# Linear attention and a GELU layer on one core: a planner that models two GpSimd stops, and a last half block in other PSUM banks

## The chip, the cores and the metric

The kernel runs on one core of one Trainium2 chip. The metric is the device time of one execution in microseconds (us), as the median of several runs. All times in the profile count from the first instruction of one profiled execution; the span is the time from its first to its last instruction. PE is TensorE, DVE is VectorE, ACT is ScalarE, POOL is GpSimd and SP is SyncE, which here issues all transfers.

## The reference

Eight batches of eight heads of linear attention (576 positions, 64 wide, 128 features) give 4608 tokens of 512 values, and these go through two matrix products with an exact GELU between them (512 to 2048 to 512):

```python
def phi(x):
    proj = np.einsum('bhsd,df->bhsf', x, w_phi)
    proj = proj - np.max(np.abs(proj), axis=-1, keepdims=True)
    return np.concatenate([np.exp(proj), np.exp(-proj)], axis=-1)
q_p, k_p = (phi(q), phi(k))
kv = np.einsum('bhsf,bhsd->bhfd', k_p, v)
z = np.sum(k_p, axis=2)
num = np.einsum('bhsf,bhfd->bhsd', q_p, kv)
den = np.einsum('bhsf,bhf->bhs', q_p, z)[..., None] + 1e-06
x = (num / den).transpose(0, 2, 1, 3).reshape(4608, 512)
h = x @ w_in
g = 0.5 * h * (1.0 + erf(h / sqrt(2)))
out = g @ w_out
```

All data are float32. The matrix products are kept accurate by splitting each operand into a high and a low part and adding three of the four partial products.

## The kernel before

**Stages.** The first part of the program mixes two things. The *attention* goes batch by batch and pair of heads by pair: `pk` and `pq` are the projections of k and q, `mx` (DVE) and `mb` (POOL, an all-reduce over partitions, line L550) their absolute maxima, `ek` and `ef` the exponentials (ACT), `kv` the sums over positions, `kvn` a copy of them, `pn` the numerators and `xo` their copy, which is written to HBM as `x_d`. The denominators go by matmuls `pd` and a copy `do` for the first two batches, and later by `un` (DVE) and an all-reduce `db` on POOL (line L592). They go to HBM as `d_d`; DVE takes their quotients in `dc`, which are written to HBM as `r_d`. The *blocks* are the two matrix products. Eight plain blocks (j = 0 to 7, 256 tokens each) load `x_d` into `xl` and `r_d` into `rb`, multiply and split them into `xh` and `xl`, and then for each of eight units u do 24 matmuls into `ph_j_u`, two GELUs on ACT, one subtraction `gl_j_u` on DVE, and 12 matmuls into `po_j`. The weights `w_i` and `w_o` are loaded as float64 bit patterns and converted on DVE (`wt_i`, `wt_o`, lines L362 to L368) during the first 200 us.

Five wide blocks (j = 4 to 8 in units of 512 tokens) then do the same with seven products for each 2 x 2 block multiplication instead of eight. Their first product goes into `pa` and `pb` and reads operands from HBM, `s_d` (sums of weights) and `o_d` (plain weights), through a ring of eight slots, two in each of the tiles `w_o0`, `w_o4`, `w_o8` and `w_o12`, which the plain blocks no longer need then (loads at line L860). The inputs of a wide block are loaded into `xr` and `wbp` (lines L807 and L811). Its second product is done for two halves m = 0 and 1. For each half, eight units add 7 x 3 matmuls into seven sums, M1 to M7, from the operands `gs` and `sp`; then the seven sums are added up into four output quarters and written out (line L963).

**PSUM.** The banks are tags of one pool: `pp` (two banks), `kv`, `pn`, `ph` (two) and `po` (two banks in one tile). The seven sums of a half block stand in `po` (M1, M2, M4, M5) and the two `pp` (M6, M7 and M3). One half must therefore be added up before the next may start in the same banks.

**What sets the order.** The function `fused_kernel` does not issue instructions; it describes operations to a planner (`Plan`), each with an engine, a cost, a rank (a due time) and its buffers. `Plan.order` then plays the program once: of the operations that can start next on each engine it takes the one of lowest rank, and sets its start and end. Instructions are issued in the order of these starts. The planner thus fixes the row of instructions of every engine, among them SP, where a transfer that must wait for its buffer holds up all that stand behind it. Due times come from constants at the end of the file: `T15` sets the pace of the blocks, `CR` and `CSPAN` when the sums of weights are due, and so on.

The planner knows that GpSimd can stop VectorE. In the kernel before, when an all-reduce starts at t, any VectorE instruction without an operand in PSUM is taken not to start before t + `LOCK_MAX` (1.4 us, for a maximum) or t + `LOCK_SUM` (2.4 us, for a sum):

```python
if o.eng == "dve" and not o.psum and taken and taken[-1][0] <= t < taken[-1][1]:
    t = taken[-1][1]
...
taken.append((t, t + (LOCK_MAX if cost < 3.0 else LOCK_SUM)))
```

All matmuls stand at line L315 of the profile, all two-operand instructions of DVE at L345, all copies on ACT at L339, since helpers record them.

## Time and profile before

| | |
|---|---|
| median of 3 runs | 1074.14 us (1073.64 to 1078.09) |
| profiled execution | 1074.69 us, of which the span is 1072.8 us |
| PE busy | 1041.4 us, 97% of the span |
| DVE / ACT / POOL busy | 827.5 (77%) / 671.6 (63%) / 327.1 (30%) us |
| mean granted clock of PE | 0.994 of full speed |

A line of the profile's timeline reads: start in us, length in us, engine, line, operation, written tile <- read tiles, shapes, number of instructions drawn together; in brackets the idle time of the engine just before it, and what ended it. The table of stretches gives, for each stretch of the span, the busy time of each engine in it. The chain of waits follows the work that ended last back through what released it; its pieces have a start, a length and a name. Tile names are shortened there: `w_o` stands for all of `w_o0` to `w_o14`.

### The profile page before, as it was taken

How to read it: one execution, taken by the hardware profiler on the slowest of the kernel's cores; microseconds unless marked ns; L12 is line 12 of the kernel's file. 1: busy time of each engine (PE TensorE's matmuls, PEld its weight loads, DVE VectorE, ACT ScalarE, POOL GpSimd, SP SyncE). 2: the span in 40 equal slices, each digit the busy share in tenths (PEclk: the TensorE clock that was granted, in tenths of full speed). 3: DMA queues.
4: the chain of work that ended last, by engine and by line, in shares of the span. 5: the costliest groups of instructions: out<-in, count | busy, mean ns of one | idle time of the engine just before them, and what ended most of it. 6: DMA issues, size and time to landing. Idle time of an engine off the chain costs nothing.

```text
span 1072.8 us, 24540 instructions
## 1 busy us (share of the span) xinstructions
PE 1041.4 (97%) x9578; PEld 911.5 (85%) x9578; DVE 827.5 (77%) x1588; ACT 671.6 (63%) x1236; POOL 327.1 (30%) x116
## 2 busy tenths in 40 slices
PE   7898999999999999999999999999999999999997
PEld 4666777778787887888788898899999999999997
DVE  5999999557787467668769869768778788787784
ACT  5997878778777777878686434444354454354351
POOL 1452045565676566676573100000000000000000
PEclk9999999999999999999999999999999999999999
DMA  7888852324214223223114771998668768766621
GB/s 274 286 295 258 268 143 88 89 70 123 76 54 134 75 68 114 68 63 96 55 48 137 194 227 47 300 284 267 207 206 262 216 201 271 217 193 207 204 78 40
DMA packets 178643, 174.33 MB, mean 162 GB/s; under 512 B 29168, under 2 KB 164784, under 8 KB 176480
## 3 DMA queue, kind: packets, MB, share of 16 engines
q1 hardware_dynamic: 178528, 172.76, 52.5%
q8 instruction: 76, 1.25, 0.5%
q14 instruction: 39, 0.32, 0.1%
HBM read 138.83 MB, written 33.89 MB: 161 GB/s over the span
## 4 chain that ended last, share of the span: by engine, by line
PE 75%; DVE 14%; DMA 5%; issue 2%; ACT 2%; SPq 1%; POOL 1%; DVEq 0%; ACTq 0%; POOLq 0%
PE po L315 29%; PE ph L315 13%; PE pb L315 10%; PE pa L315 7%; PE kv L315 5%; PE pn L315 5%; PE pk L315 4%; PE pq L315 3%; DVE tt L345 2%; DVE mx L494 1%; DVE gl L345 1%; DVE ek L345 1%; DVE wt_o L366 1%; DVE pc L345 1%; POOL db L592 1%
## 5 line engine op out<-in xcount | busy, mean ns | idle before, releaser
L592 POOL PARTITION_ALL_REDUCE db<-un x48 | 178.1, 3710 | 137.2 <-DVE un L589 117.9
L315 PE MATMUL ph<-xh,w_i 128*128 128x256 f32 x1024 | 201.3, 285 | 2.6 <-DVE gl L345 2.6
L550 POOL PARTITION_ALL_REDUCE mb<-pc x64 | 151.5, 2375 | 134.6 <-ACT pc L339 128.4
L315 PEld LDWEIGHTS ph<-xh,w_i 128*128 128x128 f32 x1024 | 163.8, 188 | 12.4 <-issue 6.7
L315 PE MATMUL po<-w_o,gh 128*128 128x512 f32 x512 | 163.5, 400 | 0.2 <-ACT ob L339 0.2
L315 PE MATMUL ph<-xl,w_i 128*128 128x256 f32 x512 | 144.3, 282 | 0.0
L315 PE MATMUL pb<-b,w_o 128*128 128x256 f32 x936 | 132.8, 282 | 2.6 <-DMA w_o<-o_d 2.2
L315 PEld LDWEIGHTS pb<-b,w_o 128*128 128x128 f32 x936 | 120.4, 190 | 3.0 <-DMA w_o<-o_d 2.4
L315 PE MATMUL po<-t,sp 128*128 128x256 f32 x720 | 110.1, 280 | 2.5 <-DVE ob L345 2.1
L315 PEld LDWEIGHTS po<-w_o,gh 128*128 128x128 f32 x512 | 90.2, 188 | 25.3 <-issue 9.1
L315 PEld LDWEIGHTS kv<-vt,ek 128*64 128x64 f32 x2560 | 85.0, 140 | 26.1 <-issue 8.9
L315 PE MATMUL pa<-b,w_o 128*128 128x256 f32 x702 | 101.8, 282 | 0.5 <-DVE gl L345 0.5
L315 PE MATMUL po<-w_o,gl 128*128 128x512 f32 x256 | 101.1, 395 | 0.0
L315 PEld LDWEIGHTS ph<-xl,w_i 128*128 128x128 f32 x512 | 96.6, 189 | 1.8
L315 PEld LDWEIGHTS po<-t,sp 128*128 128x128 f32 x720 | 95.6, 188 | 2.9 <-issue 2.3
L315 PE MATMUL kv<-vt,ek 128*64 128x65 f32 x2560 | 91.8, 226 | 4.9 <-ACT kvn L339 3.0
L345 DVE TENSOR_TENSOR g<-g 128x128 f32<-128x128 f32 x320 | 91.3, 288 | 5.9
L494 DVE TENSOR_REDUCE mx<-pk 128x4 f32<-128x512 f32 (+2 forms) x90 | 51.6, 576 | 55.8 <-PE pk L315 53.0
L502 ACT ACTIVATE ek<-ek 128x512 f32<-128x512 f32 (+1 forms) x140 | 81.8, 589 | 18.1 <-DVE ek L345 16.2
L315 PEld LDWEIGHTS pa<-b,w_o 128*128 128x128 f32 x702 | 91.3, 190 | 0.8 <-DVE gl L345 0.7
L339 ACT CAST gs<-g 128x384 fp32r<-128x384 f32 x80 | 41.0, 513 | 75.7 <-PE po L315 75.4
L556 ACT ACTIVATE ef<-pc 128x576 f32<-128x576 f32 x128 | 81.4, 679 | 10.6 <-DVE pc L345 7.4
(102 smaller groups left out, 1973.7 us busy)
## 6 DMA issues: line engine op xcount, KB each, us to landing
w_o<-s_d SPq DMA_DIRECT2D x156, 256.0 KB
w_o<-o_d SPq DMA_DIRECT2D x117, 256.0 KB
vt<-in_va_dram SPq DMA_DIRECT2D x32, 325.0 KB
kt<-in_kT_dram SPq DMA_DIRECT2D x16, 576.0 KB
qt<-in_qT_dram SPq DMA_DIRECT2D x64, 144.0 KB
x_d<-xo SPq DMA_DIRECT2D x64, 144.0 KB
out_dram<-ob SPq DMA_DIRECT2D x36, 256.0 KB
raw_i<-in_w_in_dram SPq DMA_DIRECT2D x8, 1024.0 KB
```

What stands on the lines that cost most here:

```text
L315: return tc.keep_in_program_order(nc.tensor.matmul(*a, **kw))
L339: op(eng, cost, lambda: nc.scalar.copy(out=dst(), in_=src()), r=r, w=w, **kw)
L345: op(eng, cost, lambda: e.tensor_tensor(out=dst(), in0=a(), in1=b(), op=o), r=r, w=w, **kw)
L366: op("dve", dve(1024), lambda: v.scalar_tensor_tensor(out=t(), in0=low(), scalar=29, in1=t(), op0=ALU.logical_shift_right, op1=ALU.bitwise ...
L494: op("dve", dve(128 * n * nj, True), lambda view=view, mx=mx, js=js: nc.vector.tensor_reduce(out=mx()[:, 0].rearrange("p (j i) -> p j i", ...
L502: op("act", act(256 * n, inside), lambda at=at, es=es, s=s: nc.scalar.activation(es[s](), at(), AF.Exp, scale=1.0 - 2.0 * s), r=[parts[0][ ...
L550: op("pool", 2.35, lambda mb=mb, pc=pc: nc.gpsimd.partition_all_reduce(mb(), pc(), P, bass_isa.ReduceOp.absmax), r=[pc], w=[mb], **k(1))
L556: op("act", act(2 * HS), lambda ef=ef, pc=pc, s=s: nc.scalar.activation(ef()[:, s], pc(), AF.Exp, scale=1.0 - 2.0 * s), r=[pc], w=[ef], ta ...
L592: op("pool", 3.85, lambda db=db, un=un: nc.gpsimd.partition_all_reduce(db(), un(), P, bass_isa.ReduceOp.add), r=[un], w=[db], **k())
```

## The change

**The planner's model of VectorE and GpSimd.** Each operation gets a `port`: 0 where it is not on VectorE or has an operand in PSUM, 1 otherwise, 2 for a fast instruction with a single large input (marked by a class `Fast`). An all-reduce now starts at the later of t + 0.13 and the end of a running VectorE instruction, and records two spans: in the first, from its start to 1.1 us before its end, operations of port 1 and 2 wait; in the second, from 0.85 or 0.9 to 0.2 or 0.15 us before its end, those of port 2 wait. The costs of the two all-reduces are 2.28 and 3.6 us instead of 2.35 and 3.85.

```diff
-            if o.eng == "dve" and not o.psum and taken and taken[-1][0] <= t < taken[-1][1]:
-                t = taken[-1][1]
+            if o.port and taken:
+                held = taken[-1]
+                if held[0] <= t < held[1]:
+                    t = held[1]
+                if o.port == 2 and held[2] <= t < held[3]:
+                    t = held[3]
             return t
...
+            if o.eng == "dve":
+                port[0] = o.port
             if o.eng == "pool":
-                taken.append((t, t + (LOCK_MAX if cost < 3.0 else LOCK_SUM)))
+                at = max(t + 0.13, clock["dve"] - 0.02 if port[0] else 0.0)
+                cost += at - t - 0.13
+                end = t + cost
+                taken.append((at, end - (1.11 if o.cost < 3.0 else 1.13), end - (0.85 if o.cost < 3.0 else 0.9), end - (0.2 if o.cost < 3.0 else 0.15)))
```

**A dependence.** A buffer `said` without storage makes the planner place the first wide block's first casts `gs` behind the last plain block's two output copies on ACT.

**The last half block** (j = 8, m = 1). Its seven sums stand in four banks of the tags `ph`, `ph`, `kv` and `pn`: M1 and M2, M4 and M5, M6 and M7, M3. In its last unit the products come in the order 1, 2, 6, 7, 5, 4, 3, and the sums are added up one by one as they are finished, with three output transfers instead of two.

```diff
-            po0 = ps["po"]([P, 4, TB], F32, f"po_{j}_{m}")
-            po1 = [ps["pp"]([P, 2, TB], F32, f"po_{j}_{m}_{n}") for n in range(2)]
...
+            late = j == NBLK // 2 - 1 and m == 1
+            if late:
+                banks = [ps[tag]([P, 2, TB], F32, f"po_{j}_{m}_{n}") for n, tag in enumerate(("ph", "ph", "kv", "pn"))]
+                place = {n: (banks[i // 2], i % 2) for i, n in enumerate((1, 2, 4, 5, 6, 7, 3))}
...
-                for at, n in enumerate((1, 2, 4, 5, 6, 7, 3)):
+                for at, n in enumerate((1, 2, 6, 7, 5, 4, 3) if late and u == NU - 1 else (1, 2, 4, 5, 6, 7, 3)):
...
-                    op("pe", 3 * mm_cost(128, TB), go, r=[xt, wt], w=[bank], rank=lag(u + at / 7))
+                    op("pe", 3 * mm_cost(128, TB), go, r=[xt, wt], w=[part[n]], also=[bank], rank=lag(u + at / 7))
...
+            if late:
...
+                copy("act", act(TB, True), v1, M[1], [part[1]], [v], also=k["also"], rank=k["rank"])
+                add(c11, v1, M[2], [part[2], v], [left])
...
+                add(v1, v1, M[6], [part[6], v], [v])
+                add(u3, v1, M[7], [part[7], v], [right])
+                add(v1, v1, M[5], [part[5], v], [v])
+                for i, n in ((1, 5), (0, 4)):
+                    add(lambda i=i, ob=ob: ob[1]()[:, i], u3, M[n], [part[n], right], [low])
...
+                add(u3, v1, M[3], [part[3], v, low], [right])
```

**Constants.** Some twenty due times and thresholds get other values; two of them:

```diff
-CSPAN = 106.117
+CSPAN = 147.298
-T15 = 853.69
+T15 = 848.682
```

The matmuls and their number stay the same. The order of every engine changes, since the planner plays with other costs and due times. Three places are shown, always the instructions of the kernel before and then those of the changed kernel; the line numbers of the two files differ (L315 and L329 are the same matmul helper, L345 and L359 the same DVE helper, L860 and L875 the same load).

On PE, where the first half of the last block ends and the second begins (`po_8_0` are sums of the first half, `po_8_1` of the second; the last number of a name counts buffers). Before:

```order
L315 MATMUL po_8_0_0_12899<-t_3_1_8216,sp_8_0_7_13300 128x256 x3
L315 MATMUL po_8_0_0_12899<-t_3_0_8197,sp_8_0_7_13300 128x256 x3
L315 MATMUL po_8_0_1_12935<-w_o14_2208,sp_8_0_7_13300 128x256 x3
L315 MATMUL po_8_1_0_13343<-t_0_1_7801,sp_8_1_0_13318 128x256 x3
L315 MATMUL po_8_1_0_13343<-t_0_0_7790,sp_8_1_0_13318 128x256 x3
L315 MATMUL po_8_1_0_13343<-t_0_1_7801,sp_8_1_1_13186 128x256 x3
```

After:

```order
L329 MATMUL po_8_1_0_13313<-w_o2_838,gs_8_1_0_13280 128x256 x3
L329 MATMUL po_8_1_1_13324<-t_0_1_7807,gs_8_1_0_13280 128x256 x3
L329 MATMUL po_8_1_0_13313<-w_o0_666,gs_8_1_1_13131 128x256 x3
L329 MATMUL po_8_1_0_13313<-w_o2_838,gs_8_1_1_13131 128x256 x3
L329 MATMUL po_8_0_12908<-t_3_0_8190,sp_8_0_7_13300 128x256 x3
L329 MATMUL po_8_0_0_12899<-t_3_1_8211,sp_8_0_7_13300 128x256 x3
L329 MATMUL po_8_0_0_12899<-t_3_0_8190,sp_8_0_7_13300 128x256 x3
L329 MATMUL po_8_0_1_12935<-w_o14_2159,sp_8_0_7_13300 128x256 x3
L329 MATMUL po_8_1_1_13324<-t_0_1_7807,gs_8_1_1_13131 128x256 x3
```

Products of the second half, which have banks of their own now, stand ahead of the last four of the first half.

On SP, at the change-over from the plain to the wide blocks (`xr_5` and `wbp` are inputs of the second wide block, `w_o0` to `w_o12` the ring of operands of the first). Before:

```order
L860 DMA w_o8_1699<-o_d0_379 128x2x256
L860 DMA w_o8_1699<-s_d0_7120 128x2x256
L807 DMA xr_5_0_8153<-x_d4_0_3920 128x4x32
L811 DMA wbp_94<-r_d4_0_4693 64x2x32 x2
L807 DMA xr_5_0_8153<-x_d4_1_3960 128x4x224
L811 DMA wbp_94<-r_d4_1_4803 64x2x224 x2
L807 DMA xr_5_1_8167<-x_d4_1_3960 128x4x64
L807 DMA xr_5_1_8167<-x_d5_0_4780 128x4x192
L860 DMA w_o12_2122<-o_d0_379 128x2x256
L860 DMA w_o12_2122<-o_d1_1115 128x2x256
```

After:

```order
L875 DMA w_o8_1642<-o_d0_470 128x2x256
L875 DMA w_o8_1642<-s_d0_6952 128x2x256
L875 DMA w_o12_2014<-o_d0_470 128x2x256
L875 DMA w_o12_2014<-o_d1_1019 128x2x256
L875 DMA w_o0_666<-s_d1_7101 128x2x256 x2
L822 DMA xr_5_0_8179<-x_d4_0_3778 128x4x32
L826 DMA wbp_94<-r_d4_0_4519 64x2x32 x2
L822 DMA xr_5_0_8179<-x_d4_1_3908 128x4x224
L826 DMA wbp_94<-r_d4_1_4641 64x2x224
L875 DMA w_o4_1252<-s_d1_7101 128x2x256
```

Four loads of the ring moved ahead of the loads of `xr_5_0`; the load of `w_o4` stands behind the `wbp` loads now.

On DVE, ahead of the subtraction `gl` of unit 6 of the first plain block. Before:

```order
L345 TENSOR_TENSOR ek_2_1_3_0_2009<-pk_2_1_3_1930,mx_2_1_3_1939 128x512
L364 TENSOR_SCALAR wt_o12_1895<-wt_o12_1895 128x1024
L362 TENSOR_SCALAR wt_o14_1996<-wt_o14_1996 128x1024
L366 SCALAR_TENSOR_TENSOR wt_o12_1895<-raw_o12_1701,wt_o12_1895 128x1024
L494 TENSOR_REDUCE mx_2_1_4_2067<-pk_2_1_4_2048 128x4
L586 TENSOR_SCALAR un_2_0_1_2071<-ef_2_0_1_1970,kvn_2_0_0_1368 128x288
L368 SCALAR_TENSOR_TENSOR wt_o12_1895<-raw_o12_1701,wt_o12_1895 128x1024
L586 TENSOR_SCALAR un_2_0_1_2071<-ef_2_0_1_1970,kvn_2_0_0_1368 128x288
L345 TENSOR_TENSOR pc_2_1_0_2041<-pc_2_1_0_2041,mb_2_1_0_2051 128x576
L589 SCALAR_TENSOR_TENSOR un_2_0_1_2071<-ef_2_0_1_1970,kvn_2_0_0_1368,un_2_0_1_2071 128x288
L364 TENSOR_SCALAR wt_o14_1996<-wt_o14_1996 128x1024
L345 TENSOR_TENSOR gl_0_6_2124<-ph_0_6_2023,gh_0_6_2087 128x512
```

After:

```order
L359 TENSOR_TENSOR ek_2_1_1_0_1931<-pk_2_1_1_1860,mx_2_1_1_1921 128x512
L376 TENSOR_SCALAR wt_o12_1888<-wt_o12_1888 128x1024
L378 TENSOR_SCALAR wt_o12_1888<-wt_o12_1888 128x1024
L600 TENSOR_SCALAR un_2_0_1_1976<-ef_2_0_1_1926,kvn_2_0_0_1522 128x288
L380 SCALAR_TENSOR_TENSOR wt_o12_1888<-raw_o12_1676,wt_o12_1888 128x1024
L600 TENSOR_SCALAR un_2_0_1_1976<-ef_2_0_1_1926,kvn_2_0_0_1522 128x288
L382 SCALAR_TENSOR_TENSOR wt_o12_1888<-raw_o12_1676,wt_o12_1888 128x1024
L359 TENSOR_TENSOR gl_0_6_2012<-ph_0_6_1934,gh_0_6_1996 128x512
```

The first steps of `wt_o14`, the subtraction `pc_2_1_0` and part of `un_2_0_1` moved from before this `gl` to behind it.

## Rows read from the trace of the kernel before

**Rows 1.** Stretches: from:to, length, busy us (instructions) of each engine, clock, DMA

```profile
0.00:180.00 180.00, 159.71 (x1833) 117.27 (x1834) 161.63 (x229) 146.06 (x258) 65.49 (x28) 0.98 0.72 232
180.00:660.00 480.00, 479.73 (x4373) 394.53 (x4372) 350.53 (x576) 343.59 (x570) 261.61 (x88) 1.00 0.34 99
...
150.00:180.00 30.00, 27.03 (x217) 22.30 (x218) 29.97 (x33) 24.36 (x37) 19.26 (x6) 1.00 0.40 113
...
660.00:690.00 30.00, 27.33 (x195) 25.97 (x194) 24.22 (x56) 14.78 (x34) 0.00 (x0) 0.94 0.68 203
```

**Rows 2.** Waits of PE: for what, us in total, times, longest

```profile
PE ph L315 <- DVE gl L345: 2.6, 2, 1.4
PE pn L315 <- ACT do L339: 2.4, 1, 2.4
...
PE pb L315 <- DMA w_o<-o_d: 2.2, 1, 2.2
PE po L315 <- DVE ob L345: 2.1, 1, 2.1
...
PE pa L315 <- DVE gl L345: 0.5, 1, 0.5
...
PE po L315 <- DVE sp L345: 0.4, 1, 0.4
```

**Rows 3.** Timelines of POOL, DVE and PE between 150 and 171 us

```profile
150.53 4.19 POOL L592 PARTITION_ALL_REDUCE db<-un  x1 [5.53 <-DVE un L589]
...
151.57 2.41 DVE L364 TENSOR_SCALAR wt_o<-wt_o 128x1024 uint32<-128x1024 uint32 x1
153.90 1.37 DVE L362 TENSOR_SCALAR wt_o<-wt_o 128x1024 f32<-128x1024 f32 x1
...
160.82 0.67 DVE L364 TENSOR_SCALAR wt_o<-wt_o 128x1024 uint32<-128x1024 uint32 x1
...
162.15 0.39 PE L315 MATMUL ph<-xh,w_i 128*128 128x256 f32 x1 [1.42 <-DVE gl L345]
...
170.12 0.39 PE L315 MATMUL ph<-xh,w_i 128*128 128x256 f32 x1 [1.20 <-DVE gl L345]
```

**Rows 4.** Chain of waits, 60 to 100 us: start, length, what

```profile
73.33 6.12 DMA r_d<-dc
```

**Rows 5.** Timelines of SP and PE at the change-over

```profile
652.05 0.54 SPq L860 DMA_DIRECT2D w_o<-s_d  x1
666.47 0.38 SPq L807 DMA_DIRECT2D xr<-x_d  x1
...
671.38 1.21 SPq L860 DMA_DIRECT2D w_o<-o_d  x2
...
665.40 0.39 PE L315 MATMUL po<-w_o,gl 128*128 128x512 f32 x1
```

**Rows 6.** Chain of waits, 655 to 690 us

```profile
671.38 4.99 DMA w_o<-o_d
...
677.38 2.38 PE pa L315 x12
679.76 2.08 PE pb L315 x12
...
683.99 1.42 PE pb L315 x12
```

**Rows 7.** Timeline where the last half block begins

```profile
1047.60 1.66 PE L315 MATMUL po<-t,sp 128*128 128x256 f32 x12 [2.12 <-DVE ob L345]
```

**Rows 8.** Timeline of the last unit and of the additions after it

```profile
1064.94 0.87 PE L315 MATMUL po<-w_o,gs 128*128 128x256 f32 x6
...
1066.55 0.37 ACT L339 COPY wbd<-po 128x256 f32<-128x256 f32 x1 [10.77 <-PE po L315]
...
1069.11 1.19 SPq L963 DMA_DIRECT2D out_dram<-ob  x2
1069.52 0.42 DVE L345 TENSOR_TENSOR ob<-wbd,po 128x256 f32<-128x256 f32 x1
```

More of the change, by code (lines that the diff above doesn't have):

```diff
@@ L56 @@
 class Op:
-    __slots__ = ("eng", "cost", "fn", "bufs", "rank", "table", "late", "deps", "users", "wait", "ready", "start", "end", "n", "names", "nbytes", "duty", "kind", "psum", "stream")
+    __slots__ = ("eng", "cost", "fn", "bufs", "rank", "table", "late", "deps", "users", "wait", "ready", "start", "end", "n", "names", "nbytes", "duty", "kind", "psum", "stream", "port")
 class Plan:
@@ L93, in pool, with op @@
         return lambda shape, dt, name: Buf(self, tag, lambda: make(shape, dt, name))
-    def op(self, eng, cost, fn, r=(), w=(), also=(), rank=0.0, table=None, late=0.0, kb=0, duty=1.0, kind="f", psum=False):
+    def op(self, eng, cost, fn, r=(), w=(), also=(), rank=0.0, table=None, late=0.0, kb=0, duty=1.0, kind="f", psum=False, port=None):
         r, also = ([getattr(b, "pair", b) for b in x] for x in (r, also))
@@ L98, in op @@
         o.eng, o.cost, o.fn, o.rank, o.table, o.late, o.n = eng, cost, fn, rank, table, late, len(self.ops)
+        o.port = 0 if eng != "dve" or psum else (2 if getattr(cost, "fast", False) else 1) if port is None else port
         o.users, o.ready, o.nbytes, o.duty, o.kind, o.psum, o.stream = [], self.since, kb, duty, kind, psum, self.stream
@@ L167, in order @@
         last, first = ["f"], {}
-        taken = []
+        taken, port = [], [0]
         def run(t, work, duty):
@@ L272, in mm4_cost @@
     return max(1.75 * m, 4 * (n / 2.4 + 1.5)) / 1e3
+class Fast(float):
+    fast = True
 def dve(n, psum=False, fast=False):
-    return ((62 if psum else 66) + (n / 2 if fast else n)) / 960
+    return (Fast if fast else float)(((62 if psum else 66) + (n / 2 if fast else n)) / 960)
 def act(n, psum=False):
@@ L639, in fused_kernel @@
     NU = NFC // 2
+    said = Buf(plan, None, None)
     def block(j, rank):
@@ L701, in block @@
             plan.stream = "f"
-            copy("act", act(DM, True), ob, lambda m=m: po()[:, m], [po], [ob], rank=rank(1))
+            copy("act", act(DM, True), ob, lambda m=m: po()[:, m], [po], [ob, said] if j == 2 * JW - 1 else [ob], rank=rank(1))
             op("sp", 0.06, lambda m=m, ob=ob: nc.sync.dma_start(out=out[j * TB + m * P : j * TB + (m + 1) * P, :], in_=ob()), r=[ob], kb=262, rank=rank(1))
@@ L908, in wide_block @@
             lag = lambda u: rank((LAG + 4 * m + u / 2) / NU)
[L909 to L911 removed]
+            late = j == NBLK // 2 - 1 and m == 1
+            if late:
+                banks = [ps[tag]([P, 2, TB], F32, f"po_{j}_{m}_{n}") for n, tag in enumerate(("ph", "ph", "kv", "pn"))]
+                place = {n: (banks[i // 2], i % 2) for i, n in enumerate((1, 2, 4, 5, 6, 7, 3))}
+            else:
+                po0 = ps["po"]([P, 4, TB], F32, f"po_{j}_{m}")
+                po1 = [ps["pp"]([P, 2, TB], F32, f"po_{j}_{m}_{n}") for n in range(2)]
+                place = {1: (po0, 0), 2: (po0, 1), 4: (po0, 2), 5: (po0, 3), 6: (po1[0], 0), 7: (po1[0], 1), 3: (po1[1], 0)}
+            part = {n: Buf(plan, None, lambda b=b, z=z: b()[:, z]) if late else b for n, (b, z) in place.items()}
             opens = (1, 4, 6, 3)
@@ L916, in wide_block @@
                 k = dict(rank=URGE + lag(u - 0.5))
-                late = j == NBLK // 2 - 1 and m == 1
                 gt = sb[("gh", "kt", "ef")[u % 3] if late else "gh"]([P, 2, 3, P], F32R, f"gs_{j}_{m}_{u}")
@@ L920, in wide_block @@
                 g = lambda i, G=G: (lambda: G()[:, i])
-                copy("act", act(3 * P), lambda gt=gt: gt()[:, 0], g(slice(1, 4)), [G], [gt], **k)
+                copy("act", act(3 * P), lambda gt=gt: gt()[:, 0], g(slice(1, 4)), [G, said] if (j, m) == (JW, 0) else [G], [gt], **k)
                 tt("dve", dve(3 * P), lambda gt=gt: gt()[:, 1], g(slice(1, 4)), lambda gt=gt: gt()[:, 0].bitcast(F32), ALU.subtract, [G, gt], [gt], **k)
@@ L1056 @@
 LEAD = 335.963
-HOLD = 25.318
-WR = -19.754
-ATR = 16.117
+HOLD = 26.545
+WR = -25.088
+ATR = 16.919
 T0 = 29.835
```

48 lines of the change are left out of this document (26 added, 22 removed).

## The prediction

> **What bounds the kernel now.** I read the table of 30-us stretches first. From 180 to 660 us PE is busy for 479.7 of 480 us [rows 1]; with 97% of the span busy, only its holes can be shortened, since the change keeps the same matmuls. The holes lie in three places: the start, where PE is busy for 159.7 of the first 180 us, so 20.3 us are idle (of them 3.0 in 150 to 180, where VectorE is busy for 29.97 of 30 us [rows 1]); the change-over to the wide blocks, 2.7 us in 660 to 690 [rows 1]; and the end. Next came PE's waits by what released them, which put names to them: DVE gl, ACT do, DMA w_o, DVE ob and DVE sp [rows 2]. The timelines around each of these waits then gave its cause.
>
> The three stories differ. **At the start** VectorE is the late engine, and part of its lateness is not work. The fast one-input instruction of line L364 takes 0.67 us when GpSimd is idle and 2.41 us inside a 4.19 us all-reduce; the next one, L362, is stopped again, 1.37 us for about 0.67 [rows 3]. So one all-reduce stops VectorE in two separate spans, 1.74 and 0.70 us, and between them it runs. Behind them stand the gl of units 6 and 7 of the first plain block, and PE waits for each: 1.42 us until 162.15 and 1.20 us until 170.12 [rows 3]. **At the change-over** the SP queue stands still: after the load of 652.05 its next instruction, the load of xr_5_0, waits for VectorE until 666.47, and six loads issue one after another from there. The load of w_o12 behind them goes at 671.38, although its slot is free from the last po product that reads it, which ends at 665.8 [rows 5]. It lands 4.99 us later, PE waits 2.18 us for it, and then has half its clock: twelve pa matmuls take 2.38 us and twelve pb 2.08, where twelve at full clock take 1.42 [rows 6]. **At the end** the second half (m=1) of the last block needs the banks of the first half, and PE waits 2.12 us for the additions that empty them [rows 7], besides 0.38 us for a DVE sp just before [rows 2].
>
> **The change part by part.** The sum is made against the profiled execution, 1074.69 us (1072.8 span and 1.9 around it), which is 0.55 us above the median shown.
>
> *Last half block, start.* Its sums move to four banks of other tags, which are free by then, since the last products in them stand far ahead in either order. Five of its products, of units whose operands are ready, now stand ahead of the first half's last four, twelve matmuls or 1.4 us of work at full clock [rows 6], which covers the wait for the DVE sp; nothing after them uses the banks that are being emptied. So 2.12 + 0.38 go: **-2.5**. Late next is nothing that I see, since in the timeline DVE finishes this half's operands ahead of their use.
>
> *Last half block, drain.* With t0 the start of the last unit's products, 1064.94, the copy of product 1 stood at 1066.55, that is t0 + 1.61, because it shared a tile with products 4 and 5; the six additions followed until 1069.52 + 0.42, t0 + 5.0 [rows 8]. In the changed kernel the copy waits for products 1 and 2 alone, whose six matmuls end at t0 + 0.87 [rows 8], so it begins near t0 + 0.95. From the copy to the last addition there were six steps in 2.97 us, 0.50 each [rows 8]; now there are seven, of which three do not depend on the one before them and may follow as soon as it is done, 0.42 us after its start [rows 8]: 2.9 to 3.5 us. With the last one's 0.42 the end comes at t0 + 4.3 to 4.9, the gain is 0.1 to 0.7, and I take **-0.5**, nearer the short end, since the independent ones lie in the middle of the chain. The three output transfers instead of two issue 0.6 us apart [rows 8] and only the last counts; it lands about 2 us after issue as before.
>
> *Change-over.* In the changed SP order both w_o12 loads and the w_o0 loads stand ahead of xr_5_0, so they can go when PE frees the slot, near 665.8 by the old clock, and land about 671, over 2 us ahead of the need at 674.2. That takes away the 2.2 us wait [rows 2] and, as PE no longer stands still there, the half clock: 2.38 - 1.42 + 2.08 - 1.42 = 1.6 us [rows 6]. The 0.49 us wait of pa for a DVE gl [rows 2] goes too, since four w_o12 products of po (2.8 us) now stand ahead of that pa. Together 4.3. Against it the load w_o4<-s_d of the next round now stands behind xr_5_0 and the waits of its wbp loads; if SP is held until 671 as now, it lands at 676, about when PE comes to it. I give 0.5 back: **-3.8**, between 0 (the hole moves to w_o4) and -4.3.
>
> *Start.* In the changed order the gl of unit 6 has 4.7 us less VectorE work ahead of it (each instruction at its duration without stops), the gl of unit 7 1.7 us less; the waits of 1.42 and 1.20 us [rows 3] should go, -2.6. Against this stands the chain to the first plain block: dc_0_0, from which r_d is written (6.12 us to land [rows 4]), has 4.0 us more VectorE work ahead of it, and xl_0 2.2 us more. PE has 2.4 us less work to do before ph_0_0. If all of it were exposed the first block would cost 4.0 + 2.4 = 6.4 us more; if the stops that the new spans avoid make up for it, nothing. VectorE is idle for 18 of the first 180 us [rows 1], which can take up part of the 4.0: I take 1.6 exposed, a quarter, so **-1.0** in all, from -3 to +4.
>
> *What stays out of the sum.* New due times let the attention run a little ahead of the plain blocks between 180 and 600. PE is fully busy there and the other engines have room (VectorE 350.5 of 480 us [rows 1]), so I count it as nothing; if the cover goes, what comes back is a wait of the kind of 0.5 us per block. The said dependence puts both output copies of the last plain block ahead of the first wide casts on ACT, where one stood behind two casts; PE's waits hold none for these copies that is long enough to be counted.
>
> A rule to weigh here: the trace shows the L364 instruction done after 2.41 us, 0.74 us before its all-reduce ends [rows 3]. The Trainium skill, page "SBUF — State Buffer", says of the port pair that VectorE and GpSimd share that it is an exclusive lock and that whoever starts first holds it for the whole instruction. By that rule L364 would have begun to run at the all-reduce's end, 154.72 us, and would have ended 3.8 us after its start. The trace, with 2.41 us, does not agree; what the sum would be by the rule is the fourth rival.
>
> **Sum.** -2.5 - 0.5 - 3.8 - 1.0 = -7.8: 1074.69 - 7.8 = 1066.9 in the profile's terms, 0.55 less for the median: 1066.3 us. By the ends of the terms, -2.6 - 0 + 4 gives 1075.5 and -3.2 - 4.3 - 3 gives 1063.6; a start that fills another fifth of its 20.3 us idle [rows 1] would go down to 1060.
>
> **The rivals.**
> 1. *Only the end is real.* The start gives as much as it takes, and the hole at the change-over moves from w_o12 to w_o4 or w_o8, 2.2 us plus the half clock. Then 1074.1 - 3.0 to -4 = 1070 to 1071, and with one exposed microsecond or two in the start up to 1074. For it: the changed order still has six loads that wait on VectorE in the middle of the ring. Against it: eight slots of six products at 0.71 us are 5.7 us of work, more than the 4.99 us that a load takes.
> 2. *Slower: the first block comes later.* The chain dc_0_0, r_d, rb, xl_0 sets when ph_0_0 can start, and before it PE has little else. Place: 55 to 100 us. Price: 6.4 us as above, a half-clock stretch of 1.6 us where PE waits, and 4.0 us once more for the second half's quotient dc_0_1, which stands behind the same instructions: 12.0, against the -3.0 of the end: 1083. It decides from 8.4 us more idle in the first 120 us. For it: the wait of 2.4 us on ACT do [rows 2] shows that PE has no cover there. Against it: VectorE is idle for 18 of the first 180 us [rows 1], and idle time ahead of dc_0_0 takes up work that comes earlier.
> 3. *The planner's spans change nothing.* PE waits for VectorE in only 2.6 + 2.1 + 0.5 + 0.4 us [rows 2]; if the stops merely fall on other instructions, the start stays and the change-over is luck: 1067 to 1071, between the forecast and rival 1.
> 4. *The shared port as a whole-instruction lock.* If a stop lasted to the all-reduce's end, instructions put between the two spans would lose another 0.74 us at each of the six all-reduces of 150 to 180, 4.4 us: 1066.3 + 4.4 = 1070.7. It is the rule named above. The two rows of [rows 3] speak against it.
>
> **How the numbers follow.** Forecast 0.55 (1062 to 1068.7), rival 1 0.20, rival 2 0.10, rival 3 0.12 (half of it under 1068.8), rival 4 0.03. A measurement of this kernel tells about 0.5%, 5.4 us, from no change: faster lies below 1068.8, slower above 1079.5. Faster: 0.55 + 0.06 and a little of rival 1, 0.65; slower: 0.09 of rival 2; same 0.26. The range leaves out rival 2 and the upper end of rival 1 and 3: 1060 to 1074.5.
>
> **What would show it.** Right: no wait of po on DVE ob near 1045 and the last product within 2.7 us of the last output's issue; no PE hole and no half clock between 655 and 690, with the w_o12 load issued before xr_5_0; no wait of ph on DVE gl between 150 and 175. Wrong: PE's idle time before 120 us larger by over 3 us, a wait of pa or pb on w_o4 or w_o8 near 670, or new waits of PE on ACT between 180 and 600, of which there are nearly none now.

## The result and the profile after

The changed kernel takes 1082.05 us in the median (1080.70 to 1084.92), the kernel before 1073.56 in the same comparison: 1.0084 times as long, with a 95% interval of 1.0064 to 1.0103. So it is slower by 0.84%, 9 us, where 1066.3 had been forecast. The profiled execution has a span of 1079.3 us, 6.5 more than before.

The page of the changed kernel, its total and PE's row, and its table of stretches (columns as in [rows 1]):

```profile
span 1079.3 us, 24544 instructions
...
PE 1045.2 (97%) x9578; PEld 911.8 (84%) x9578; DVE 832.7 (77%) x1589; ACT 661.3 (61%) x1230; POOL 333.2 (31%) x116
```

```profile
0.00:180.00 180.00, 158.59 (x1789) 113.66 (x1790) 160.00 (x230) 149.40 (x261) 70.49 (x29) 0.98 0.72 231
180.00:660.00 480.00, 474.99 (x4347) 389.10 (x4346) 353.00 (x565) 327.70 (x555) 262.71 (x87) 1.00 0.34 99
150.00:180.00 30.00, 29.09 (x251) 22.75 (x250) 28.82 (x35) 26.28 (x42) 21.75 (x7) 1.00 0.38 105
660.00:690.00 30.00, 27.75 (x195) 25.66 (x193) 23.61 (x51) 13.77 (x30) 0.00 (x0) 1.00 0.47 133
690.00:720.00 30.00, 29.86 (x241) 29.89 (x242) 17.69 (x45) 10.69 (x28) 0.00 (x0) 0.94 0.91 287
```

Between 180 and 660, where [rows 1] had 479.73 us of PE, there are 474.99 now: 5 us of idle time where there was 0.3. From 150 to 180 PE gained 2 us of the 2.6 that were forecast. The largest waits of PE (columns as in [rows 2]):

```profile
PE pd L329 <- ACT xo L353: 6.8, 4, 5.7
PE kv L329 <- ACT ek L516: 4.6, 5, 1.9
PE pn L329 <- ACT do L353: 3.2, 5, 1.6
PE pq L329 <- DVE ek L359: 2.3, 5, 0.6
...
PE pa L329 <- DMA w_o<-o_d: 2.2, 1, 2.2
PE pq L329 <- ACT pc L353: 1.9, 2, 1.5
```

The waits of po on DVE ob and sp and of ph on DVE gl [rows 2] are gone. The waits of the attention's matmuls (kv, pn, pd, pq) have grown. The kernel before has such waits too, but nearly all of them ahead of 180 us. Between 180 and 570 us its only wait is the first line here; the others are the largest of the changed kernel's there, 4.8 us in all:

```profile
PE po L315 <- ACT ob L339: 0.2, 1, 0.2
```

```profile
PE pq L329 <- DVE ek L359: 1.6, 4, 0.6
PE pq L329 <- ACT pc L353: 1.5, 1, 1.5
```

Idle time does not show all of it, since PE is busy while its matmuls run slower than they can. So I worked out a **lost time**: for each kind of matmul (same shapes, same tiles) I took the median distance from its start to the start of the next, in the kernel before; the lost time up to t is t less these distances summed over all matmuls that started before t. It ends with the last matmul. In us, by stretch, for all kernels of this study (one profiled execution each):

```
kernel           0-180  180-570  570-660  660-750  750-end   sum
before            39.2    22.1      1.1      5.3      2.3    70.0
after             40.2    32.3      0.3      5.0     -0.9    76.9
tail_only         40.5    22.2      1.0      4.4     -0.9    67.2
after_oldmodel    38.5    31.1      1.6     12.3     -0.8    82.7
after_oldconsts   43.1    31.4      1.0      5.1     -0.8    79.8
after_margin      41.3    31.2      2.6     14.1      0.4    89.6
tail_patience     39.8    22.2      0.7      4.9     -0.8    66.8
tail_wr           36.2    30.4      0.3      4.4     -0.9    70.4
before_copy       29.8    20.8      0.9      6.0      3.5    61.0
after_copy        38.5    20.7      0.1      5.2     -0.9    63.6
after_dc3         37.5    32.5      0.3      6.3      0.6    77.2
after_long        43.3    76.7      9.2      2.8     -0.4   131.6
after_long2       37.4    20.6      0.0      5.4     -0.9    62.5
before_long2      32.6    21.0      1.2      4.3      3.7    62.8
tail_xr5_14       37.3    21.8      1.6      7.2     -0.9    67.0
tail_xr5_20       39.8    22.1      0.7     10.7     -0.1    73.2
tail_lessdve      36.1    21.7      0.8      2.7     -0.9    60.4
after_slowpool    42.2    23.0      1.5     13.9     -0.8    79.8
```

The second line less the first is +1.0, **+10.2**, -0.8, -0.3 and -3.2, together 6.9; the spans differ by 6.5, since the additions behind the last matmul got shorter. The first column is not sharp: five later kernels with the order of the kernel before up to 180 us (tail_only, tail_patience, both tail_xr5 and tail_lessdve) have 36.1 to 40.5 there. The second is: the four of them that keep that order to 570 us (all but tail_patience) have 21.7 to 22.2, and the kernel before 22.1.

**The middle, in the changed kernel.** The timelines of POOL, DVE and PE at one of these places, and a pair of pq in the open (first line):

```profile
80.44 0.76 PE L329 MATMUL pq<-qt,wbd 64*128 64x288 f32 x4
```

```profile
341.52 2.26 POOL L564 PARTITION_ALL_REDUCE mb<-pc  x1 [0.75 <-ACT pc L353]
...
341.71 1.85 DVE L359 TENSOR_TENSOR pc<-pc,mb 128x576 f32<-128x576 f32 x1
...
343.14 0.75 PE L329 MATMUL pq<-qt,wbd 64*128 64x288 f32 x2
...
343.92 0.42 DVE L359 TENSOR_TENSOR ek<-pk,mx 128x256 f32<-128x256 f32 x1
...
344.50 0.72 PE L329 MATMUL pq<-qt,wbd 64*128 64x288 f32 x2 [0.60 <-DVE ek L359]
```

VectorE's pc takes 1.85 us instead of 0.74, because the all-reduce that began 0.19 us earlier stops it. Behind it on VectorE stands the ek that frees a PSUM bank, and PE's second pq needs that bank. The wait is 0.60 us, but the loss is twice that. Four matmuls of a pair, two for each half of the rows, take 0.69 us from the first start to the next matmul when both banks are free, for then the halves run side by side; here they run one after the other and take 2.00. Between 180 and 570 us the groups of pq that are drawn out so cost 7.3 us in the changed kernel (ten groups) and 0.5 in the kernel before (one).

**The start.** The timelines of DVE, ACT and PE at the largest hole:

```profile
82.93 0.18 DVE L628 TENSOR_TENSOR dc<-dp 128x18 f32<-128x18 f32 x1 [3.87 <-DMA r_d<-dc]
...
88.00 1.21 DVE L382 SCALAR_TENSOR_TENSOR wt_o<-raw_o,wt_o 128x1024 uint32<-128x1024 uint32 x1
...
89.24 1.04 ACT L353 CAST w_o<-wt_o 128x1024 fp32r<-128x1024 f32 x1 [5.62 <-DVE wt_o L382]
90.19 0.39 ACT L353 COPY xo<-pn 128x288 f32<-128x288 f32 x1
...
90.64 1.19 PE L329 MATMUL pd<-ef,kvn 128*32 128x288 f32 x8 [5.67 <-ACT xo L353]
```

The quotient dc_0_1 stands at the head of VectorE's queue and waits 3.87 us until the transfer r_d<-dc has read the buffer that it is to write. Behind it are the steps of wt_o; ACT waits for the last of them in front of the copy xo; and PE waits for that copy, 5.67 us, where the longest wait of the kernel before was 2.4 [rows 2].

**The change-over.** The timelines of SP and PE:

```profile
673.39 3.78 SPq L875 DMA_DIRECT2D w_o<-o_d  x2
...
678.59 0.55 SPq L822 DMA_DIRECT2D xr<-x_d  x1
...
686.52 1.23 SPq L875 DMA_DIRECT2D w_o<-o_d  x2
...
690.14 1.62 PE L329 MATMUL pa<-b,w_o 128*128 128x256 f32 x6 [2.23 <-DMA w_o<-o_d]
```

The w_o12 loads go ahead of xr, and the wait of [rows 2] at w_o12 is gone. But at 690 us PE waits 2.23 us for another load of the ring. The changed kernel is 10 us behind by then, so this is some 3 us after the place of the old wait, which ended at 676.4. The half clock follows there too: the granted clock is 0.94 for 690 to 720, and 0.52 in its first 3 us:

```profile
690.00:693.00 3.00, 2.86 (x13) 2.90 (x14) 2.26 (x9) 0.89 (x2) 0.00 (x0) 0.52 1.08 371
```

**The end.** The timeline of the last unit, as in [rows 8]:

```profile
1071.83 0.87 PE L329 MATMUL po<-w_o,gs 128*128 128x256 f32 x6
...
1072.74 0.37 ACT L353 COPY wbd<-po 128x256 f32<-128x256 f32 x1 [9.80 <-PE po L329]
...
1075.84 0.42 DVE L359 TENSOR_TENSOR ob<-wbd,po 128x256 f32<-128x256 f32 x1
1076.29 0.33 SPq L988 DMA_DIRECT2D out_dram<-ob  x1
```

With t0 = 1071.83 the copy begins at t0 + 0.91 and the last addition ends at t0 + 4.43, where it was t0 + 5.0.

### The profile page after: what moved, and what is told of

Same layout as the page of the kernel before. It is cut to its first block, busy times and chain, and to the rows that moved or that the text cites. A ratio compares the mean times of both kernels' runs of the same rounds, so it can differ in the third digit from the quotient of the medians.

```text
span 1079.3 us, 24544 instructions
## 1 busy us (share of the span) xinstructions
PE 1045.2 (97%) x9578; PEld 911.8 (84%) x9578; DVE 832.7 (77%) x1589; ACT 661.3 (61%) x1230; POOL 333.2 (31%) x116
## 4 chain that ended last, share of the span: by engine, by line
PE 70%; DVE 16%; ACT 5%; POOL 3%; DMA 3%; issue 3%; SPq 1%; DVEq 0%; POOLq 0%; ACTq 0%
PE po L329 29%; PE ph L329 12%; PE pb L329 10%; PE pa L329 8%; PE pn L329 3%; PE kv L329 3%; POOL db L606 3%; DVE pc L359 2%; PE pk L329 2%; PE pq L329 2%; DVE un L603 2%; DVE un L600 2%; DVE mx L508 2%; DVE ek L359 1%; ACT ek L516 1%
## 5 line engine op out<-in xcount | busy, mean ns | idle before, releaser
L606 POOL PARTITION_ALL_REDUCE db<-un x48 | 182.5, 3803 | 110.4 <-DVE un L603 81.4
L329 PE MATMUL ph<-xh,w_i 128*128 128x256 f32 x1024 | 198.4, 284 | 0.0
L329 PEld LDWEIGHTS ph<-xh,w_i 128*128 128x128 f32 x1024 | 163.1, 188 | 11.0 <-issue 7.6
L329 PE MATMUL po<-w_o,gh 128*128 128x512 f32 x512 | 163.8, 401 | 0.0
L329 PE MATMUL ph<-xl,w_i 128*128 128x256 f32 x512 | 144.2, 282 | 0.0
L329 PE MATMUL pb<-b,w_o 128*128 128x256 f32 x936 | 131.6, 281 | 0.2 <-DMA w_o<-s_d 0.2
L329 PEld LDWEIGHTS pb<-b,w_o 128*128 128x128 f32 x936 | 119.7, 189 | 0.4 <-DMA w_o<-s_d 0.4
L329 PEld LDWEIGHTS po<-w_o,gh 128*128 128x128 f32 x512 | 89.8, 188 | 24.4 <-issue 8.8
L329 PE MATMUL po<-t,sp 128*128 128x256 f32 x720 | 109.0, 280 | 0.0
L329 PEld LDWEIGHTS kv<-vt,ek 128*64 128x64 f32 x2560 | 83.8, 137 | 25.8 <-ACT ek L516 7.7
L329 PE MATMUL pa<-b,w_o 128*128 128x256 f32 x702 | 101.5, 282 | 2.7 <-DMA w_o<-o_d 2.2
L516 ACT ACTIVATE ek<-ek 128x512 f32<-128x512 f32 (+1 forms) x140 | 81.8, 589 | 36.1 <-DVE ek L359 34.0
L329 PE MATMUL po<-w_o,gl 128*128 128x512 f32 x256 | 101.0, 395 | 0.0
L329 PEld LDWEIGHTS ph<-xl,w_i 128*128 128x128 f32 x512 | 96.6, 189 | 1.7
L329 PEld LDWEIGHTS po<-t,sp 128*128 128x128 f32 x720 | 95.3, 189 | 0.0
L329 PE MATMUL kv<-vt,ek 128*64 128x65 f32 x2560 | 88.9, 223 | 5.9 <-ACT ek L516 4.6
L359 DVE TENSOR_TENSOR g<-g 128x128 f32<-128x128 f32 x320 | 90.1, 288 | 5.6
L329 PEld LDWEIGHTS pa<-b,w_o 128*128 128x128 f32 x702 | 91.1, 189 | 3.3 <-DVE g L359 2.4
L359 DVE TENSOR_TENSOR gl<-ph,gh 128x512 fp32r<-128x512 f32 x64 | 43.9, 686 | 53.6 <-ACT ph L698 53.3
```

Source lines behind the costliest of these rows:

```text
L329: return tc.keep_in_program_order(nc.tensor.matmul(*a, **kw))
L359: op(eng, cost, lambda: e.tensor_tensor(out=dst(), in0=a(), in1=b(), op=o), r=r, w=w, **kw)
L516: op("act", act(256 * n, inside), lambda at=at, es=es, s=s: nc.scalar.activation(es[s](), at(), AF.Exp, scale=1.0 - 2.0 * s), r=[parts[0][ ...
L606: op("pool", 3.6, lambda db=db, un=un: nc.gpsimd.partition_all_reduce(db(), un(), P, bass_isa.ReduceOp.add), r=[un], w=[db], **k())
```

## The experiments

**Which part of the change?** The last half block alone; the changed kernel with the old model; with the old constants; and planned with more room for PE.

```diff
# tail_only: the kernel before, with the last half block of the changed kernel
# after_oldmodel: the changed kernel, and
+            if o.eng == "dve" and not o.psum and taken and taken[-1][0] <= t < taken[-1][1]:
+                t = taken[-1][1]
+                taken.append((t, t + (LOCK_MAX if cost < 3.0 else LOCK_SUM)))   # 2.35, 3.85
# after_oldconsts: the changed kernel, and CR ... ATR as in the kernel before
# after_margin: the changed kernel, and
-MARGIN = 0.8
+MARGIN = 1.6
```

> The kernel before with the new last half block alone (banks, order of the last unit, drain); instructions before the last half block stand as before. All theories agree: the lost time of PE up to 1040 us is that of before, the 2.1 us wait on DVE ob and the 0.4 us wait on DVE sp are gone, and the drain is 0.5 us shorter. 3.0 us faster than before, about 1070.5 us. If it is not, the last half block itself is part of what made the changed kernel slow.

> The changed kernel with the old planner model (one span, all-reduces at 2.35 and 3.85 us); the new constants, the said dependence and the last half block stay. Theory M (the two-span model and the shorter all-reduce costs make the plan place attention too tightly, and PE pays in 180 to 570): the 10 us lost there come back, about 1072 us. Theory K (the new constants do it, by pulling the attention ahead): about 1082, lost time in 180 to 570 still near 32 us. Theory F (constants and model are fitted to each other, and any mixture loses): 1080 or more.

> The changed kernel with the constants of the kernel before; the two-span model, the new all-reduce costs, the said dependence and the last half block stay. Theory M: the loss in 180 to 570 stays near 32 us, about 1082 us. Theory K: it falls to about 22 us, about 1071. Theory F: 1080 or more, as the other mixture.

> The changed kernel, planned with 1.6 us instead of 0.8 between the end of another engine's operation and the PE operation that needs it. If PE's waits in 180 to 570 come from plans that are tighter than the chip is (theories M and K alike), PE's second pq of a pair no longer waits for its bank and the loss in 180 to 570 falls by 4 us or more, to 1078 or less. If the waits come from the queues of VectorE and GpSimd being late by more than that, or from another plan as such (theory F), it stays at 1080 or more.

tail_only: 1068.97 us against 1075.67, ratio 0.9949 (0.9931 to 0.9967); its span is 3.4 us shorter, and 3.2 us of lost time are gone at the end. The last half block does what it was forecast to do. after_oldmodel: 1087.80, ratio 1.0129 (1.0101 to 1.0158). after_oldconsts: 1085.94, 1.0110 (1.0082 to 1.0137). Either mixture loses 31 us in 180 to 570. Going back on the model alone or on the constants alone does not bring the 10 us back, so theories M and K fall in the form in which they were put. The mixtures lose at other places, though: in after_oldmodel the groups of pq cost 1.5 us instead of 7.3, and PE waits 3.2 us for gl. They do not show what model and constants each do in the changed order. after_margin: 1095.91, 1.0198 (1.0171 to 1.0224), 31.2 there too, so that more room between an operation and its matmul does not help.

**Does any other order lose?** Two single constants, each on top of tail_only.

```diff
# tail_patience
-PATIENCE = 0.486
+PATIENCE = 0.451
# tail_wr
-WR = -19.754
+WR = -25.088
```

> The kernel before with the new last half block, and one constant more: PATIENCE 0.486 becomes 0.451, as in the changed kernel. 684 rows of PE's order differ from the 1247th of 3652 on (near 245 us), none ahead of it. Theory F (the order of the kernel before is a selected one; any other order that the planner draws makes PE wait in the attention): lost time between 245 and 570 us grows by 3 us or more over the 16 of the kernel before, and the time is 1072 or more. Theories M and K (something in the model or in the due times of the weights and the attention): no more than 1 us, 1069 to 1070.

> The same with one other constant, WR -19.754 becomes -25.088 (when the weights' conversion is due). 2098 rows of PE's order differ, from the 447th on (near 35 us). Theory F: PE loses 5 us or more in 180 to 570 beside whatever the start gives or takes; 1074 or more. Theory K with this constant as the cause: as the changed kernel, +10 in 180 to 570. Theory M: no loss in 180 to 570, about 1070.

tail_patience: 1070.03, ratio 0.9954 (0.9936 to 0.9972), 22.2 us lost in the middle as before: theory F in its strict form falls, since 684 other rows cost nothing. tail_wr: 1074.33, 0.9993 (0.9977 to 1.0009), 30.4 in the middle, near what theories F and K both had. Of the 8.3 us more than before, 5.8 lie between 180 and 210, where one wait stands with a lower clock behind it (0.89 for that stretch; waits of PE, 180 to 570 us):

```profile
PE ph L320 <- DVE gl L350: 3.4, 1, 3.4
```

So an order can be as good as the old one, or cost several us. What of this the planner sees can be read from the end that `Plan.order` returns for its own plan: 1049.3 us for tail_only, 1049.9 for tail_patience, 1053.9 for tail_wr, 1053.2 for the kernel before, 1062.2 and 1064.5 for after_oldconsts and after_oldmodel, and 1050.7 for the changed kernel. The first six of these run 20 to 24 us longer on the chip than that, the changed kernel 31. The larger part of what the mixtures lose thus stands in their own plans, and the loss of the changed kernel does not: it was planned 2.5 us shorter than the kernel before.

**Is it GpSimd?** The same orders with each all-reduce replaced: by a copy, and by a copy and one-element memsets that make it about as long.

```diff
# before_copy, after_copy
-nc.gpsimd.partition_all_reduce(mb(), pc(), P, bass_isa.ReduceOp.absmax)
+nc.gpsimd.tensor_copy(out=mb(), in_=pc())
# after_long (16 and 29 memsets), after_long2 and before_long2 (10 and 19)
+        return [keep(nc.gpsimd.tensor_copy(out=to(), in_=src())), *[keep(nc.gpsimd.memset(to()[:, 0, :1], 1.0)) for _ in range(n)]]
```

> The kernel before, same order, with every all-reduce of GpSimd replaced by a copy of its input (the maxima and the denominators are left out, so this is only a look at time). The stops of VectorE and the latency of GpSimd mostly go. Theory S (PE's waits in 180 to 570 come from stops and from GpSimd's length): nothing to gain here, since this kernel has hardly a wait there; 22 us lost in 180 to 570 stays at 21 to 22. The start loses 3 us or so less.

> The changed kernel, same order, with the same replacement. Theory S: the 10 us that the changed order loses more than the kernel before in 180 to 570 fall to 2 or less, since nothing is late any more. Theory O (the changed order itself has PE instructions too close behind ACT and VectorE work, whatever GpSimd does): 5 us or more of the difference stay.

> The changed kernel in the same order, with each all-reduce replaced by a copy and then a row of one-element memsets, about as long together as the all-reduce (2.3 and 3.6 us; maxima and denominators are left out). GpSimd is as late as in the changed kernel, but hardly stops VectorE. Theory S1 (PE's 10 us in 180 to 570 come from VectorE's stops): lost time in 180 to 570 falls to 23 to 25 us, as with short copies (21.6). Theory S2 (they come from the length of GpSimd's own chain, pc to mb to ef and un to db): it stays at 30 or more.

> As after_long, with fewer memsets (10 and 19), so that the copy and its memsets last as long as the all-reduces did, about 2.2 and 3.6 us (maxima and denominators are left out). Theory S1 (VectorE's stops make PE's 10 us in 180 to 570): lost time there 22 to 25 us. Theory S2 (GpSimd's length does, the stops being a part of it only where they delay what GpSimd needs): 28 us or more.

> The same replacement in the order of the kernel before. Theory S1 and S2 both: 21 to 23 us lost in 180 to 570, as this order had no waits with the real all-reduces. If it loses 5 us or more there, the replacement itself disturbs (tiny instructions on GpSimd), and after_long2 has to be read against it.

The stretch from 180 to 570 us of four kernels (columns as in [rows 1]): the changed kernel, after_copy, after_long2 and the kernel before:

```profile
180.00:570.00 390.00, 384.99 (x3771) 308.34 (x3770) 290.03 (x444) 292.22 (x493) 258.29 (x86) 1.00 0.29 86
```

```profile
180.00:570.00 390.00, 390.00 (x3844) 315.69 (x3841) 236.35 (x463) 297.46 (x500) 69.28 (x87) 1.00 0.33 92
```

```profile
180.00:570.00 390.00, 390.00 (x3810) 315.53 (x3809) 241.79 (x464) 297.66 (x499) 200.43 (x1362) 1.00 0.33 93
```

```profile
180.00:570.00 390.00, 389.81 (x3798) 314.59 (x3797) 274.87 (x429) 302.74 (x499) 253.19 (x86) 1.00 0.28 83
```

With copies the changed order loses 20.7 us in the middle instead of 32.3, the order before 20.8 instead of 22.1: the difference of 10 us is GpSimd's. after_copy takes 1064.87 (0.9895, 0.9861 to 0.9929), before_copy 1068.72 (0.9938, 0.9917 to 0.9958); before_copy gains 9.4 in the start, where 3 had been expected. after_long missed its aim: a memset with its gap takes 0.15 us, so the replaced maxima lasted 3.1 us and the sums 5.0, and it lost 76.7 in the middle (1135.17, 1.0571, 1.0551 to 1.0591). It shows how far PE depends on GpSimd's length once that grows by more than a third. after_long2 hits it (0.66 + 10 x 0.15 = 2.2 and 0.66 + 19 x 0.15 = 3.5 us): 20.6 in the middle, 1064.47 (0.9904, 0.9874 to 0.9935). before_long2 loses 21.0 (1068.29, 0.9946, 0.9928 to 0.9963). GpSimd is as late in after_long2 as in the changed kernel: between 180 and 570 us the replaced maxima last 2.29 us in the median and the sums 3.87, the all-reduces 2.27 and 3.67. But it stops VectorE for 15 us in all instead of 86 (the excess of every instruction of VectorE over the duration that a fifth of its kind do not exceed, where it is over 0.1 us). So the **stops** make the 10 us, not GpSimd's length: S1. Without them the changed order is 3.8 us faster than the order before (1064.47 against 1068.29), about what the last half block gives; with them it is slower. The same shows beside the plans: with copies the changed order and the order before take 14.2 and 15.5 us more than their plans, with the all-reduces 31.4 and 20.4.

**Would a more careful cost have helped?**

```diff
# after_slowpool: the changed kernel, and
-            op("pool", 2.28,
+            op("pool", 2.8,
-            op("pool", 3.6,
+            op("pool", 4.4,
```

> The changed kernel, planned with all-reduces of 2.8 and 4.4 us instead of 2.28 and 3.6. Theory P (the plan of the changed kernel takes GpSimd for faster than it is on the chip, where it waits for VectorE and VectorE for it; a plan that takes it for slower leaves the attention time): lost time in 180 to 570 falls by 4 us or more, to 28 or less. Theory F2 (a plan's luck with the stops is not set by a cost): 30 or more again, 1080 or more.

The middle falls from 32.3 to 23.0, as theory P has it, with 72 us of stops in all. The time hardly does: 1081.05, 1.0060 (1.0037 to 1.0084), since this order loses 13.9 from 660 to 750, most of it at two new waits (waits of PE, 655 to 725 us):

```profile
PE pa L329 <- ACT b L353: 4.4, 1, 4.4
PE pb L329 <- DMA w_o<-s_d: 4.1, 1, 4.1
```

Its plan already ended at 1066.9 us, 16 later than that of the changed kernel.

**The hole at the start.**

```diff
# after_dc3: the changed kernel, and in the pool of SBUF buffers
-bufs=bufs)[:, :n]
+bufs=3 if tag == "dc" else bufs)[:, :n]
```

> The changed kernel in the same order on every engine, with three buffers instead of two for the small tiles dp and dc of the quotients. In the changed kernel VectorE stands still for 3.87 us until 82.93 in front of the sum into dc_0_1, because its buffer is that of dc_0_0, which the transfer r_d<-dc still reads; behind it stand steps of w_o4 for which ACT waits in front of a copy xo, and PE waits 5.67 us for that copy. Theory Q (this buffer is the cause of the hole at 85): VectorE's wait goes and PE's hole shrinks by 2 to 4 us; lost time of PE at 120 us falls from 34.7 to 31 or 32; 1079 us. Theory D (the chain through dc_0_0 and r_d to the first block is late as such, as the second rival of the prediction says): the hole stays over 5 us or another wait takes its place before 100 us; 1082.

Theory Q: VectorE does dc_0_1 at 79.14 without a wait, and PE's hole is 2.29 us (timelines of DVE and PE):

```profile
79.14 0.17 DVE L628 TENSOR_TENSOR dc<-dp 128x18 f32<-128x18 f32 x1
```

```profile
93.03 1.19 PE L329 MATMUL pd<-ef,kvn 128*32 128x288 f32 x8 [2.29 <-ACT xo L353]
```

The lost time falls to 32.8 at 120 us and 37.5 at 180 (changed kernel: 34.7 and 40.2). So the buffer made the wait, and most of the hole went with it. In the time nothing is seen of it: 1081.81, ratio 1.0074 (1.0054 to 1.0093), where theory Q had 1079. In the profiled execution 1.3 us of it went at the change-over and 1.5 after it. A gain of 2 to 3 us lies within what the start varies by, so whether a microsecond gained here reaches the end stays open.

**The change-over.** Loads of the ring ahead of those of xr_5, by a dependence in the planner; and less work for VectorE.

```diff
# tail_xr5_14, tail_xr5_20: tail_only, and (ring: the loads of the first wide block in order)
+                if j == JW + 1:
+                    plan.gate = [*gate, ring[14]]      # ring[20]
# tail_lessdve: tail_only, and in output_sums
-                    ... lambda to=to: to[0]()[:, to[1]], ...
+                    ... lambda to=to: to[0]()[:, to[1]][:, :8], ...
```

> The kernel before with the new last half block, and six loads of the ring (w_o12 twice, w_o0 twice, w_o4 twice) ahead of the loads of xr_5_0 on SP, as the changed kernel has the first four; nothing differs ahead of 650 us. Theory H (the hole moves: SP still has to pass the loads of xr_5 and wbp, which wait for VectorE, in the middle of the ring): the 2.2 us wait at 674 goes, another wait for w_o comes some 10 us later, and the time is within 1.5 us of the 1069 of tail_only. Theory G (the hole goes): 4 us less, 1065.

> The same with the loads of xr_5_0 behind twelve loads of the ring, by when their buffer has long been freed by VectorE, so that SP need not wait in front of them. Theories H and G agree here: no wait for w_o over 0.5 us between 655 and 720, no half clock there, lost time of PE between 660 and 720 falls from 4.3 to 1 or less, 1065 us. If a hole is left here too, SP's order is not what makes it.

> The kernel before with the new last half block, the 32 subtractions of the sums t, which VectorE does between 620 and 700 us, cut to 8 of 256 columns (part of the sums is left out): about 8 us of VectorE's work less there, same order. Theory V (the change-over loses its 4 us because VectorE is full from 640 to 670, and any order of loads only moves the place): lost time of PE between 660 and 720 falls from 4.3 to 1.5 or less, 1066 us. Theory L (it is the loads' latency, about 5 us each, in a ring of eight): it stays at 3.5 or more, 1069.

tail_xr5_14: 1070.95, 0.9975 (0.9961 to 0.9989). The hole moved, as H has it, but not to another load of the ring, and the time is 2.0 us above tail_only's 1068.97, not within 1.5. It is now a wait on ACT, whose copy ob waits for the transfer of the ob before it, and that stands on SP behind the loads of xr_5 (timelines of ACT and PE):

```profile
680.98 0.58 ACT L344 COPY ob<-po 128x512 f32<-128x512 f32 x1 [3.97 <-DMA out_dram<-ob]
```

```profile
681.62 1.65 PE L320 MATMUL po<-w_o,gs 128*128 128x256 f32 x6 [4.06 <-ACT ob L344]
```

tail_xr5_20: 1076.82, 1.0028 (1.0015 to 1.0042). From 660 to 690 it loses 3.8 us, as tail_only does (3.7), and 7 more between 720 and 750, among them a 2.2 us wait of pb for w_o<-s_d; both theories had expected a gain, and both were wrong. The planner had this one: its plan ends at 1054.2, 4.9 us after that of tail_only. tail_lessdve: 1064.41, 0.9908 (0.9877 to 0.9939); of its gain over tail_only 4.4 us lie in the start, which this edit does not touch, and 1.7 at the change-over, where the waits of PE from 655 to 725 are these (tail_only, then tail_lessdve):

```profile
PE pb L320 <- DMA w_o<-o_d: 2.7, 2, 2.2
```

```profile
PE pb L320 <- DMA w_o<-o_d: 1.4, 1, 1.4
```

2.7 us of lost time stay, between what V and L had expected: VectorE's load looks like a part of the change-over's loss, on one profiled execution each, and the rest is not settled.

## Why the prediction was wrong

*What stays out of the sum* is the step that failed. It said that new due times and another order between 180 and 600 cost nothing, since PE is fully busy there and the other engines have room. They cost 10.2 us, more than the 7.8 that were forecast to be gained. Even its hedge, waits of 0.5 us per block, is 4 us for eight blocks, and no bound of the range has it. That PE did not wait there before was no sign of room. It was a property of that order: VectorE was stopped for 62 us between 180 and 570, and hardly a wait of PE came of it. In the changed order it was stopped for 70 us there, and the 10 us came of it, as after_long2 shows. VectorE's share of busy time says little on this: a stop of 1 us counts where PE waits for a bank behind it. Two of the named signs came, more lost time ahead of 120 us (by 3.7) and new waits on ACT.

*Start.* The first half held: both waits of ph on gl went, and the stretch from 150 to 180 gained 2.1 us of PE. The second half held in kind: the transfer of dc_0_0 began at 76.60 instead of 73.33, and a hole grew, but by another way than the second rival's, a buffer of dc held by that transfer for 6.24 us, with two queues behind it. In all +1.0 instead of -1.0; the difference is less than this stretch varies by.

*Change-over.* The w_o12 wait and its half clock went: from 660 to 686 us the kernel before lost 4.9 us, the changed one 0.3. At another load, from 686 to 700, 4.4 came back: in all -0.3 instead of -3.8. It is the hole and the price of the first rival, which had 0.20.

*Last half block.* This held, mechanism and size. The start was forecast at -2.5 and the lost time, which ends with the last matmul, fell by 3.2. The drain was forecast at -0.5, between 0.1 and 0.7, and gave 0.57.

*Rival 3*, that the new spans change nothing, is nearest to what the model did. The spans themselves are about right. By their ends less their usual lengths, most of the stopped instructions of VectorE go on 1.0 to 1.1 us before a maximum's end and 1.2 before a sum's, and some fast ones only 0.1 to 0.2 before either; the change has 1.11 and 1.13, 0.2 and 0.15. But VectorE stands still for 85.7 us in the changed kernel and for 81.1 in the one before; with the old constants and the new spans it is 96.4, with the new constants and the old span 76.9.

It is not chance from run to run. In the kernel before and in tail_only, both tail_xr5 and tail_lessdve, which have its order there, the same 428 instructions of VectorE stand between 180 and 570 us, and 62.0 of 62.1 us of stops fall on the same ones. It is the plan that misses: the spans are 0.7 to 2.5 us long, and in either kernel about a third to a half of the 86 all-reduces there begin ahead of another instruction of VectorE than in the plan. That a plan that hits them would lose less was not tried.

*Rival 4*, the lock for the whole instruction, is ruled out by the times at which VectorE goes on. *Rival 2*, the slower one, has a time close to the measured one, 1083, but by luck: it wanted 8.4 us more idle time in the first 120 us, where 3.7 were lost, and had nothing in the middle.

The best kernel of the study that computes the whole result is tail_only, 0.9949 of the kernel before and 1.3% faster than the changed one: the last half block, with the old planner and its constants. tail_patience, at 0.9954, is the same within the intervals.

## What to carry to other kernels

Where a program orders the instructions, a stretch without waits is a result of that order and not a margin: price a new order there with the waits that the same engines cause elsewhere, and keep an edit that can be made alone (here the last half block) apart from a new plan. A model of a short stop that is right need not lower the stops; check what a plan does by the stops and waits in the trace of its run. Compare the end that each plan gives itself with the time on the chip: an order whose gap is much larger than that of its neighbours, here 31 us against 20 to 24, may have lost to something that the planner does not have right, here the stops. At a change-over that several queues share, count a removed wait as a gain only when the next load, the next copy and the busiest engine there have been priced too.

## What the runs showed of the hardware

Two matmuls on different halves of the rows (64 x 128 each, 288 columns) begin 0.01 us apart when their banks are free, so that a pair of pq takes 0.69 us from its first start to the next matmul. In the changed kernel, at 343 us, the second half had to wait 0.60 us for its bank, and the pair took 2.00: the wait cost 1.3.

GpSimd's all-reduce (128 x 576 in float32, 2.3 us for a maximum, 3.6 for a sum) stops VectorE in two spans: the first ends 1.0 to 1.2 us before the all-reduce does, the second, met by casts and tensor_scalar instructions alone, 0.1 to 0.2 before. A copy of the same tile (0.66 us) and one-element memsets (0.15 us each with the gap) of the same total length stop it for a sixth of the time, 15 us against 86.

The same order is stopped at the same places: in five executions 62.0 us of stops between 180 and 570 us fell on the same instructions, though four of them were 0.6 to 3.6 us ahead of or behind the first by then.

A 9 KB transfer from SBUF to HBM (r_d<-dc, 18 values in each partition) took 6.24 us from its issue until its buffer was free again, longer than the 256 KB loads of the ring, whose issue and landing took 4.99 [rows 6].
